# Issue order of the sixteen small matmuls of a tiled DFT stage: column type by column type instead of row tile by row tile

## The chip, the cores and the metric

The kernel runs on one core of one Trainium2 chip. The metric is device time in microseconds (us) of one execution; less is better. Engine names: PE is TensorE (matmuls), PEld its weight loads, DVE is VectorE, ACT is ScalarE, POOL is GpSimd, SP is SyncE, which here only issues transfers. L323 is line 323 of the kernel.

## The reference

```python
def reference(x, filt_r, filt_i, w_gate, w_val, w_out):       # x: 8 batches x 3008 x 256
    X = np.fft.rfft(x, axis=1)
    y = np.fft.irfft(X * (filt_r + 1j * filt_i)[None], n=3008, axis=1)
    t = y.reshape(8 * 3008, 256).astype(np.float32)            # 24064 tokens
    return (np.maximum(t @ w_gate, 0) * (t @ w_val)) @ w_out   # 256 -> 1536 -> 256
```

## The kernel before

A spectral filter along the sequence is followed by a gated feed-forward network (FFN). The kernel spreads the FFN over 564 steps of 1.30 us, each with two matmuls into `psV`, two into `psG` and four into `psO`, and hangs the filter's work for the next batches between these steps. For batches 2 to 7 the filter's first DFT (stage A) is "tiled": POOL loads a chunk of x (`load_chunk`), folds it by symmetry into four half-size inputs (`fold_chunk`, one for each of four column types c), and TensorE does sixteen small fp32 matmuls, one for each pair of row tile q and column type c (`tiled_a`). Each batch has four chunks j, so there are 24 such blocks.

```python
def fold_chunk(b, j):                                   # POOL
    xp = XP[j]
    t = fs.tile([128, 2, 512], FP32, tag="fold", bufs=2, name="fold")
    tt = nc.gpsimd.tensor_tensor
    tt(t, xp[:, 0:2], xp[:, 2:4], op=ALU.add)                        # L309
    tt(xp[:, 2:4], xp[:, 0:2], xp[:, 2:4], op=ALU.subtract)          # L310
    tt(xp[:, 0], t[:, 0], t[:, 1], op=ALU.add)                       # L311: input of c = 0
    tt(t[:, 0], t[:, 0], t[:, 1], op=ALU.subtract)                   # L312: c = 1
    tt(t[:, 1], xp[:, 2], xp[:, 3], op=ALU.add)                      # L313: c = 2
    tt(xp[:, 2], xp[:, 2], xp[:, 3], op=ALU.subtract)                # L314: c = 3
    fold[b, j] = (xp[:, 0], t[:, 0], t[:, 1], xp[:, 2])

def tiled_a(b, j):
    banks = [ps.tile([128, 2, D], FP32, tag=t, name="psF") for t in ("psv", "psg", "fft", "fft")]
    for q in range(4):
        r = 32 * q
        for c in range(4):
            nc.tensor.matmul(banks[q][32 * c:32 * c + 32], WF[r:r + 24, c, :],     # L323
                             fold[b, j][c][r:r + 24], start=True, stop=True,
                             tile_position=(r, 32 * c))
    ...                                  # banks 0, 2 are copied by ACT, 1, 3 by DVE, then stored
...
def load_d(b, z0=0, z1=NZ):              # inputs of the last DFT (stage C), on SP
    for z in range(z0, z1):
        dC = sb.tile([NROW, 8, D], BF16, tag="dC", bufs=6)
        for e in range(2):
            nc.sync.dma_start(dC[48 * e:48 * e + 48], ...)                         # L427
...
# where a batch's work is hung among the FFN steps (e: offset of the four blocks)
for j, e in enumerate((-74, -69, -64, -57)):
    l = (22, 34, 34, 46)[j] if b == 2 else end - 113 + NFT * j
    def next_x(b=b, j=j, l=l):
        hold_gpsimd(yTs[l // NFT + 1][:, 0, 0:8])
        load_chunk(b, j)
        if j:
            fold_chunk(b, j - 1)
        if j == 3:
            fold_chunk(b, j)
    at_step(l, next_x)
    at_step(end + e, lambda b=b, j=j: tiled_a(b, j))
```

## Time and profile before

| | before |
|---|---|
| three timed runs, us | 902.16, 902.18, 902.97 (median 902.18) |
| the run whose trace was taken, us | 897.66, span 895.9, mean granted clock 0.997 |
| PE busy; its share of the chain that ended last | 98%; 84% |
| stage A (psF) in that chain | 3% of the span |
| one stage-A block, first psF start to next psV start | 1.07 us (chunks 0, 2), 1.26 us (chunks 1, 3) |

The execution that was traced took 4.5 us less than the timed ones. "Busy" says which engine could be the bound, the chain says that it is. The time of a single block has to be read from the timeline, because the profile models a matmul's end, as its page says, and only the starts are used here.

### The profile page before, as it was taken

How to read it: one execution, taken by the hardware profiler on the slowest of the kernel's cores; microseconds unless marked ns; L12 is line 12 of the kernel's file. 1: busy time of each engine (PE TensorE's matmuls, PEld its weight loads, DVE VectorE, ACT ScalarE, POOL GpSimd, SP SyncE). 2: the span in 40 equal slices, each digit the busy share in tenths (PEclk: the TensorE clock that was granted, in tenths of full speed). 3: DMA queues.
4: the chain of work that ended last, by engine and by line, in shares of the span. 5: the costliest groups of instructions: out<-in, count | busy, mean ns of one | idle time of the engine just before them, and what ended most of it. 6: DMA issues, size and time to landing. Idle time of an engine off the chain costs nothing.

```text
span 895.9 us, 19186 instructions
## 1 busy us (share of the span) xinstructions
PE 881.8 (98%) x7206; PEld 510.3 (57%) x7206; DVE 569.3 (64%) x873; ACT 499.4 (56%) x891; POOL 363.6 (41%) x361
## 2 busy tenths in 40 slices
PE   7899999999999999999999999999999999999998
PEld 2335555566556665556655666555655566666665
DVE  2636865577665776567766677657766577655553
ACT  3475565556555556555655565555565556555553
POOL 4351399138661376415672167801868000000001
PEclk9999999999999999999999999999999999999999
DMA  9998448534465435463375433763346512241111
GB/s 247 287 230 168 108 141 185 124 82 116 124 155 130 115 104 137 129 139 98 99 176 130 99 101 105 181 133 85 111 139 154 117 32 82 67 88 36 37 30 54
DMA packets 114098, 109.17 MB, mean 122 GB/s; under 512 B 20359, under 2 KB 98599, under 8 KB 113366
## 3 DMA queue, kind: packets, MB, share of 16 engines
q1 hardware_dynamic: 90294, 80.10, 34.6%
q0 software_dynamic: 22992, 26.41, 12.4%
q10 hardware_dynamic: 720, 1.45, 0.4%
q8 instruction: 56, 0.92, 0.4%
q14 instruction: 36, 0.29, 0.1%
HBM read 61.93 MB, written 49.81 MB: 125 GB/s over the span
## 4 chain that ended last, share of the span: by engine, by line
PE 84%; POOL 6%; issue 4%; DMA 3%; DVE 1%; ACT 1%; SPq 0%; POOLq 0%; DVEq 0%
PE psV L467 25%; PE psO L486 25%; PE psG L467 24%; PE psF L323 3%; PE psY L451 2%; PE psD L394 2%; PE psX L364 1%; DMA Fti<-in_filt_i_dram 1%; POOL XP L296 1%; POOL fold L309 1%; POOL XP L310 1%; POOL XP L605 1%; DMA Dbuf<-dsb 1%; PE psJ L520 1%; POOL XP L300 1%
## 5 line engine op out<-in xcount | busy, mean ns | idle before, releaser
L472 DVE SCALAR_TENSOR_TENSOR prod<-psG,vsb 128x512 bf16<-128x512 f32 x564 | 389.2, 690 | 265.9 <-ACT vsb L470 259.1
L470 ACT CAST vsb<-psV 128x512 bf16<-128x512 f32 x564 | 332.1, 589 | 266.1 <-PE psV L467 226.9
L467 PE MATMUL psV<-yT,WvT 128*128 128x512 bf16 x1128 | 336.4, 379 | 0.3 <-ACT vsb L470 0.3
L486 PE MATMUL psO<-WoT,prod 128*128 128x256 bf16 x2256 | 336.4, 273 | 0.0
L467 PE MATMUL psG<-yT,WgT 128*128 128x512 bf16 x1128 | 335.3, 379 | 0.8 <-ACT dsb L401 0.3
L486 PEld LDWEIGHTS <-prod 128*128 128x128 bf16 x2256 | 220.6, 98 | 143.4
L467 PEld LDWEIGHTS <-WgT 128*128 128x128 bf16 x1128 | 110.0, 98 | 135.8 <-issue 2.4
L467 PEld LDWEIGHTS <-WvT 128*128 128x128 bf16 x1128 | 98.4, 98 | 42.1 <-issue 30.8
L258 POOL CAST scr<-yT 128x8 f32<-128x8 bf16 x25 | 4.7, 190 | 263.4 <-ACT yT L456 263.4
L509 POOL DMA_DIRECT2D out_dram<-osb x5 | 2.6, 536 | 196.1 <-ACT osb L499 196.1
L380 DVE TENSOR_TENSOR tt<-psX,Ftr 128x512 bf16<-128x512 f32 x96 | 65.1, 683 | 7.4 <-PE psX L364 7.4
L499 ACT COPY osb<-psO 128x512 f32<-128x512 f32 x92 | 53.9, 586 | 27.4 <-PE psO L486 25.7
L309 POOL TENSOR_TENSOR fold<-XP 128x1024 f32<-128x1024 f32 x24 | 56.5, 2355 | 21.5 <-PE psF L323 20.4
L380 DVE TENSOR_TENSOR uu<-psX,Fti 128x512 bf16<-128x512 f32 x89 | 60.6, 681 | 0.0
L401 ACT CAST dsb<-psD 128x512 bf16<-128x512 f32 x96 | 51.5, 589 | 12.4 <-PE psD L394 12.2
L296 POOL DMA_DIRECT2D XP<-in_x_dram x96 | 56.7, 596 | 1.6 <-issue 0.8
L310 POOL TENSOR_TENSOR XP<-XP 128x1024 f32<-128x1024 f32 x24 | 56.3, 2348 | 1.9
L330 DVE CAST asb<-psF 128x512 bf16<-128x512 f32 x48 | 30.9, 686 | 19.2 <-PE psF L323 14.1
L330 ACT CAST asb<-psF 128x512 bf16<-128x512 f32 x48 | 25.8, 589 | 29.0 <-PE psF L323 29.0
L456 ACT CAST yT<-psY 128x512 bf16<-128x512 f32 x47 | 27.6, 586 | 24.9 <-PE psY L451 24.7
L458 DVE CAST yT<-psY 128x512 bf16<-128x512 f32 x47 | 32.0, 681 | 9.7 <-PE psY L451 9.7
L451 PE MATMUL psY<-M,dC 96*128 96x94 bf16 (+18 forms) x604 | 37.5, 198 | 0.5 <-DMA dC<-Dbuf 0.4
(69 smaller groups left out, 508.2 us busy)
## 6 DMA issues: line engine op xcount, KB each, us to landing
at<-Abuf SPq DMA_DIRECT2D x32, 384.0 KB
dC<-Dbuf SPq DMA_DIRECT2D x64, 192.0 KB
XP<-in_x_dram POOLq DMA_DIRECT2D x48, 256.0 KB, 6.0
Dbuf<-dsb SPq DMA_DIRECT2D x23, 512.0 KB
XP<-in_x_dram POOLq DMA_DIRECT2D x96, 96.0 KB, 2.7
Abuf<-asb SPq DMA_DIRECT2D x96, 96.0 KB
out_dram<-osb SPq DMA_DIRECT2D x69, 94.0 KB
XF<-in_x_dram SPq DMA_DIRECT2D x15, 256.0 KB
```

Source lines behind the costliest of these rows:

```text
L296: nc.gpsimd.dma_start(xp[r:r + 24, 0:4:2, :], _ap(x, (b * N1 * N2 + o) * D, [[N2 * D, 24], [47 * N2 * D, 2], [1, 512]]))
L309: tt(t, xp[:, 0:2], xp[:, 2:4], op=ALU.add)
L310: tt(xp[:, 2:4], xp[:, 0:2], xp[:, 2:4], op=ALU.subtract)
L330: copy(asf[:, :, q, :], banks[q])
L380: nc.vector.tensor_tensor(p, psX, filt, op=ALU.mult)
L401: nc.scalar.copy(dsb[:, a, o:o + 2, :], psD[a])
L451: nc.tensor.matmul(psY[:, o:o + w], dCs[b, n2 // 8][:, n2 % 8, h * 128:(h + 1) * 128], M1[:, n1:n1 + w], start=True, stop=True)
L467: nc.tensor.matmul(pt[:, :W], w[:, h, ft * 128:(ft + 1) * 128], yt[:, h, :], start=(h == 0), stop=(h == 1))
L470: nc.scalar.copy(vsb, psV[:, :W])
L472: nc.vector.scalar_tensor_tensor(prod, in0=psG[:, :W], scalar=0.0, in1=vsb, op0=ALU.max, op1=ALU.mult)
L486: nc.tensor.matmul(psO[:, t % 2], prods[ft][:, t * 128:(t + 1) * 128], WoT[:, ft, :], start=(ft == 0), stop=(ft == NFT - 1))
L499: copy(osb[:, t0 % 2:t % 2 + 1], psO[:, t0 % 2:t % 2 + 1])
```

## The change

The intent, as far as the change itself tells it, is to let consecutive matmuls go to different row tiles, so that no row tile's bank has to be filled before the next begins. The two loops are exchanged and nothing else:

```diff
-        for q in range(4):
-            r = 32 * q
-            for c in range(4):
+        for c in range(4):
+            for q in range(4):
+                r = 32 * q
                 nc.tensor.matmul(banks[q][32 * c:32 * c + 32], WF[r:r + 24, c, :],
                                  fold[b, j][c][r:r + 24], start=True, stop=True,
                                  tile_position=(r, 32 * c))
```

## The prediction

> **What bounds the kernel now.** I read the page's busy shares first, then the chain that ended last, then everything recorded for the changed line (L323, the matmuls of tiled stage A, output psF), and last the timeline of single stage-A blocks. From the page, busy time by engine and the chain by engine and line:
>
> ```profile
> PE 881.8 (98%) x7206; PEld 510.3 (57%) x7206; DVE 569.3 (64%) x873; ACT 499.4 (56%) x891; POOL 363.6 (41%) x361
> ...
> PE 84%; POOL 6%; issue 4%; DMA 3%; DVE 1%; ACT 1%; SPq 0%; POOLq 0%; DVEq 0%
> ```
>
> TensorE is the bound: 98% busy and 84% of the chain. The chain's second line gives psF 3% of the span, about 27 us, so a nanosecond less in a stage-A block is a nanosecond less at the end. But even a stage A that cost nothing would give only 3%. All that is recorded for L323:
>
> ```profile
> L323 PE MATMUL psF<-XP,WF x384: 584/587/612, 131.0 to 696.5; 24*32 24x512 f32 x192
> ...
> L323 PE MATMUL psF<-fold,WF x384: 587/600/612, 131.0 to 696.5; 24*32 24x512 f32 x192
> L323 PEldq EVENT_SEMAPHORE  x72: 51/51/727, 128.9 to 695.9; - x72
> ```
>
> 768 records for 24 blocks (6 batches, 4 chunks each) of 16 matmuls: each fp32 matmul is two passes of some 590 ns. Run one after the other, a block would take 32 x 0.59 = 19 us; it does not. The timeline of PE for a block of chunk 0, then one of chunk 1 (start us, duration, what):
>
> ```profile
> 240.41 0.61 PE L323 MATMUL psF<-XP,WF 24*32 24x512 f32 x1
> 240.42 0.62 PE L323 MATMUL psF<-fold,WF 24*32 24x512 f32 x2
> ...
> 240.51 0.94 PE L323 MATMUL psF<-XP,WF 24*32 24x512 f32 x2
> ...
> 240.96 0.59 PE L323 MATMUL psF<-XP,WF 24*32 24x512 f32 x1
> 241.48 0.60 PE L467 MATMUL psV<-yT,WvT 128*128 128x512 bf16 x2
> ...
> 248.09 0.61 PE L323 MATMUL psF<-XP,WF 24*32 24x512 f32 x1
> ...
> 248.13 0.67 PE L323 MATMUL psF<-XP,WF 24*32 24x512 f32 x2
> 248.22 0.62 PE L323 MATMUL psF<-fold,WF 24*32 24x512 f32 x2
> ...
> 248.36 0.62 PE L323 MATMUL psF<-fold,WF 24*32 24x512 f32 x2
> ...
> 248.83 0.59 PE L323 MATMUL psF<-XP,WF 24*32 24x512 f32 x1
> 249.35 0.60 PE L467 MATMUL psV<-yT,WvT 128*128 128x512 bf16 x2
> ```
>
> In the first block all 16 first passes start within 0.10 us (240.41 to 240.51, under 7 ns apart), the second pass of the last tile starts at 240.96, and the next matmul of the FFN at 241.48: 1.07 us from first to next. The old order already runs all 16 tiles at once. The second block takes 249.35 - 248.09 = 1.26 us, because its first passes come in three clumps: there is a hole after 248.13 and another after 248.24. Every block of chunks 0 and 2 looks like the first, every one of chunks 1 and 3 like the second, except the last two of the first of the six batches. Its last block:
>
> ```profile
> 158.64 0.61 PE L323 MATMUL psF<-XP,WF 24*32 24x512 f32 x1
> ...
> 159.37 0.69 PE L323 MATMUL psF<-XP,WF 24*32 24x512 f32 x2
> ...
> 160.75 0.61 PE L467 MATMUL psV<-yT,WvT 128*128 128x512 bf16 x2
> ```
>
> Here three tiles start at 158.64, and the fourth (column type 3 of row tile 0) waits until 159.37 for POOL's last fold step (L314, which starts at 158.06 and takes 1.26). The 12 tiles of the other rows stand behind it.
>
> [...] four tiles of one row group start under 7 ns apart, each with its own weight load. [...] in the last block nothing passes the tile that waits. [...] here the step is 6.7 ns (0.10 us over 15). [...]
>
> **The change part by part.** Nothing is added or removed: the same 384 matmuls, weight loads, copies and transfers. The comparison of the two programs shows the same instructions on every engine, with the waits moved.
>
> *Blocks of chunks 0 and 2, 12 of them.* Two extra semaphore instructions (51 ns each) stand ahead of row tiles 0 and 1, and both run long before the block starts (238.9 and 239.5 for the block at 240.41). Nothing stalls, 16 starts remain 16 starts: gain 0 for the 11 that have their data.
>
> *Blocks of chunks 1 and 3.* These have four such instructions, one at the first tile of each row, because these tiles wait for two things (their rows' load, and the last user of the bank). For the block at 248.09 the first two run ahead; the last of the four is at 248.2, inside the block. So the two holes are the semaphore instructions of row tiles 2 and 3: 248.13 to 248.22 and 248.24 to 248.36, together 1.26 - 1.07 = 0.19 us. In the old order they come after 8 and 12 matmuls, in the new one after 2 and 3. The old order shows that the queue gets at least four matmuls (and the second instruction after them) ahead of the array, so all four should run ahead and the block become 1.07 us. Five batches with two such blocks: 10 x 0.19 = 1.9 us, all on TensorE's path.
>
> *First batch.* POOL bounds its last two blocks, so what its second block saves is lost in the third's wait. For the last block, the new order puts all tiles of column type 3 at the end: when POOL is done at 159.37, 4 tiles are left instead of 13. The end is then 159.37 + 3 x 0.007 + (241.48 - 240.51 = 0.97) = 160.36 instead of 160.75: 0.39 us, which contains what the block before it gives (4 tiles instead of 13 behind its wait, an estimated 0.16).
>
> *What moves the other way.* Bank 0 is now finished with the 13th tile, not the 4th: its copy by ACT starts about 0.06 us later (9 x 6.7 ns). The next user of that bank is the second FFN step after the block, and the copy ends some 0.5 us ahead of it: free. POOL's loads of the next chunk wait for TensorE at more of their transfers, on a use a whole batch earlier: free.
>
> Sum: 1.9 + 0.4 = 2.3 us of 902.18, so **about 900.0 us**, 0.25% faster.
>
> **The rivals.** (1) *The stalls move with the instructions.* If what held the semaphore instruction in the old order is [...] something that clears only when the block starts, they stall after 2 and 3 tiles just as they did after 8 and 12. Then only the first batch gains: 901.8. For it: the third instruction came at 248.2 though its load was long done, and I can only guess why. Against: the second ran ahead behind four full matmuls. (2) *Serial weight loads.* If tiles of one column group share a path for weights, four in a row would load one after the other, at 27 ns (the distance of the two loads of one tile in a raw record): 16 x 27 = 0.43 us instead of 0.10 until all have started, 24 x 0.33 = 8 us, so 910. Against: the old order also has loads of two row groups in one column within 2 ns of each other. (3) [...] If the old order were serial within a row group, it would save much more; the starts 7 ns apart rule it out. (4) *PSUM or ACT becomes the bound*: the 0.06 us delay is too small against 0.5 us of slack.
>
> **Range and chances.** I give the main line some 65%, rival 1 or a half of it 25%, slower starts 8%. The runs before spread from 902.16 to 902.97, so the upper edge must hold an unchanged kernel: 899.0 to 902.8. No rival reaches 2% (18 us): faster 0.01, same 0.97, slower 0.02.
>
> **What would show it.** Right: blocks of chunks 1 and 3 take 1.07 us from first psF start to next psV start, with 16 starts under 7 ns apart and all four semaphore instructions before the first; those of chunks 0 and 2 are unchanged at 1.07; the last block of the first batch ends about 1.0 us after POOL's step. Wrong: holes after the second and third start (rival 1), starts 27 ns apart (rival 2), or TensorE idle before psV of the second step after a block (rival 4).

The forecast's sum is 1.9 + 0.4 = 2.3 us, and its 6.7 ns for each further tile are the 0.10 us of the block at 240.41 over 15 starts. The words cut from the first rival gave the author's guess of what else might hold the instruction up: how much stands ahead of it, which e3_positions tests.

## The result, and the profile after

In the first set the unchanged kernel took a median of 902.17 us (902.16, 902.18, 902.97 and 901.29), the changed one 897.91 (897.68, 900.4, 896.73, 898.15). The ratio is 0.9957, 95% interval 0.9934 to 0.998: the same within 2%. A ratio here is the mean time of one kernel's fast runs over the mean of the other's of the same rounds, so not quite the quotient of the medians. The predicted 900.0 was 2.1 too high, and 897.91 lies below the range.

First comes the page of the changed kernel, busy time and the chain by engine:

```profile
PE 871.2 (97%) x7086; PEld 507.4 (57%) x7206; DVE 569.3 (64%) x873; ACT 499.3 (56%) x891; POOL 364.4 (41%) x361
...
PE 75%; POOL 6%; issue 5%; DVE 4%; DMA 4%; ACT 4%; SPq 0%; POOLq 0%; DVEq 0%; ACTq 0%
```

Here is a trap. PE seems to have lost 10 us of work and 9 points of the chain. But the count fell from 7206 to 7086 matmuls while the weight loads stayed at 7206: 120 matmul records are missing from this trace, and where one is missing the chain takes another way, over ACT and DVE (4% each of the chain, where they had 1% each). Nothing was saved there. The blocks have to be read instead. This is the timeline of PE over the same chunk-1 block that the prediction shows (start us, duration, what):

```profile
248.23 0.63 PE L323 MATMUL psF<-XP,WF 24*32 24x512 f32 x4
248.25 0.66 PE L323 MATMUL psF<-fold,WF 24*32 24x512 f32 x8
248.31 0.98 PE L323 MATMUL psF<-XP,WF 24*32 24x512 f32 x8
248.71 0.63 PE L323 MATMUL psF<-fold,WF 24*32 24x512 f32 x8
248.76 0.61 PE L323 MATMUL psF<-XP,WF 24*32 24x512 f32 x4
249.30 0.39 PE L467 MATMUL psV<-yT,WvT 128*128 128x512 bf16 x1
```

From 248.23 to 249.30 are 1.07 us, where it was 1.26. The merged rows follow the column types, as the new order has them: four tiles of c = 0, eight of c = 1 and 2, then c = 3 together with its second passes. The two holes are gone. The cause is in what is recorded for L323 in this block, in the kernel before and then in the changed kernel (durations are least, median and greatest in ns, then first and last start):

```profile
L323 PEldq EVENT_SEMAPHORE  x4: 51/51/555, 246.1 to 248.2; - x4
```

```profile
L323 PEldq EVENT_SEMAPHORE  x4: 51/51/556, 246.2 to 247.7; - x4
```

Before, the last of the four semaphore instructions started at 248.2, inside the block that had begun at 248.09. Now it starts at 247.7, ahead of the first matmul at 248.23. In the raw records the second, third and fourth start 1.36, 0.70 and 0.58 us ahead; before, the second, with four tiles ahead of it, came 1.34 us ahead, and the third and fourth, with 8 and 12, came 0.02 and 0.16 us after the block's start. All ready blocks of the changed kernel, of whichever chunk, take 1.073 to 1.074 us.

So the predicted mechanism is there, and still the two traced executions differ by 0.3 us only (spans 895.9 and 895.6), while the timed runs differ by 4. Dividing the span at fixed points of TensorE's work shows where the traces differ:

| stretch | before | after |
|---|---|---|
| start to first tiled block | 131.00 | 130.99 |
| first to fifth block (the first batch of tiled blocks) | 109.41 | 109.57 |
| fifth block to the psV after the last (the other 20 blocks) | 456.62 | 455.80 |
| from there to the start of TensorE's last weight load | 194.21 | 194.21 |
| from there to the end | 4.62 | 5.06 |

The stretch with 20 blocks saved 0.8 us instead of 1.9, the first batch nothing, and the tail lost 0.4. That left three questions: is the timed gain of 4 us real, what gives back 1.1 us among the 20 blocks, and what happens in the first batch?

The first batch depends on a load. This is the timeline of POOL at the fold of the batch's last chunk, before and after:

```profile
149.16 2.35 POOL L309 TENSOR_TENSOR fold<-XP 128x1024 f32<-128x1024 f32 x1 [0.94 <-DMA XP<-in_x_dram]
```

```profile
149.68 2.35 POOL L309 TENSOR_TENSOR fold<-XP 128x1024 f32<-128x1024 f32 x1 [1.46 <-PE psF L323]
```

The bracket is POOL's idle time and what ended it. The second line names PE, but that matmul was long done; the semaphores of the trace show that the last piece of the x chunk landed at 149.44 and released POOL. POOL bounds the last two blocks of this batch: in the kernel before, TensorE idled 1.3 and 0.6 us in them until POOL's L314. A later start of this fold is passed on in full: in e5_new_forced, an experiment below that holds POOL up, it starts 1.45 us later than in the changed kernel's trace (151.13 against 149.68), and the psV behind the batch's last block 1.44 us later (162.32 against 160.88). The traced run of before, the only one I had when I predicted, was an early one.

The given-back 1.1 us is one wait. This is the timeline of PE around 572 us, first in the kernel before, then in the changed kernel; psY is the first work of stage C that uses the fifth batch's `dC`:

```profile
573.71 0.42 PE L451 MATMUL psY<-M,dC 96*128 96x4 bf16 x7
```

```profile
572.56 0.27 PE L451 MATMUL psY<-M,dC 96*128 96x4 bf16 x3
573.72 0.30 PE L451 MATMUL psY<-M,dC 96*128 96x94 bf16 x4 [0.89 <-DMA dC<-Dbuf]
```

Seven matmuls that ran together before now come as three and four, with a wait for the load in between. The load is issued by SP in eight pieces; here is SP's timeline for it, before and after:

```profile
568.19 3.93 SPq L427 DMA_DIRECT2D dC<-Dbuf  x8
```

```profile
568.31 4.93 SPq L427 DMA_DIRECT2D dC<-Dbuf  x8
```

The eight issues took 3.93 us before and 4.93 after; the raw records show that one took 1.20 us instead of 0.46. Beside it lies a fetch of instructions, 16 KB, 0.96 us long: it starts 2.29 us after the first of the eight issues, where it came at 4.58, after all eight, in the kernel before. The page lists its queue as q8, instruction, with 56 packets and 0.92 MB, so 16 KB each. That they bring TensorE's program is inferred: 14,412 of the 19,186 instructions on the page of the kernel before are matmuls and weight loads. Whether such a fetch holds others up is what the experiments had to show.

### The profile page after: what moved, and what is told of

Its sections match the earlier page's. It is cut to its first block, busy times and chain, and to the rows that moved or that the text cites. A ratio compares the mean times of both kernels' runs of the same rounds, so it can differ in the third digit from the quotient of the medians.

```text
span 895.6 us, 19081 instructions
## 1 busy us (share of the span) xinstructions
PE 871.2 (97%) x7086; PEld 507.4 (57%) x7206; DVE 569.3 (64%) x873; ACT 499.3 (56%) x891; POOL 364.4 (41%) x361
## 3 DMA queue, kind: packets, MB, share of 16 engines
q10 hardware_dynamic: 720, 1.45, 0.5%
## 4 chain that ended last, share of the span: by engine, by line
PE 75%; POOL 6%; issue 5%; DVE 4%; DMA 4%; ACT 4%; SPq 0%; POOLq 0%; DVEq 0%; ACTq 0%
PE psG L467 23%; PE psO L486 22%; PE psV L467 21%; DVE prod L472 4%; ACT vsb L470 3%; PE psF L323 2%; PE psD L394 2%; PE psX L364 1%; DMA XP<-in_x_dram 1%; DMA Ftr<-in_filt_r_dram 1%; PE psY L451 1%; POOL XP L296 1%; DMA dC<-Dbuf 1%; POOL fold L309 1%; POOL XP L310 1%
## 5 line engine op out<-in xcount | busy, mean ns | idle before, releaser
L467 PE MATMUL psG<-yT,WgT 128*128 128x512 bf16 x1107 | 330.8, 379 | 6.7 <-ACT dsb L401 0.6
L467 PE MATMUL psV<-yT,WvT 128*128 128x512 bf16 x1030 | 315.2, 380 | 0.3 <-ACT vsb L470 0.3
L258 POOL CAST scr<-yT 128x8 f32<-128x8 bf16 x25 | 4.7, 189 | 262.2 <-ACT yT L456 262.2
```

What stands on the lines that cost most here:

```text
L467: nc.tensor.matmul(pt[:, :W], w[:, h, ft * 128:(ft + 1) * 128], yt[:, h, :], start=(h == 0), stop=(h == 1))
```

## The experiments

Sixteen kernels ran, all with correct results. The ratios are against the unchanged kernel on the same chip; for the e6 runs those were in the main made some minutes earlier, in the set of e4 and e5.

| kernel | chip | median, us (low to high, runs) | ratio (95% interval) |
|---|---|---|---|
| e0_unchanged | 12 | 901.34 (898.05–902.8, 6) | 1.0014 (0.9997–1.0031) |
| e1_changed_again | 12 | 898.17 (897.79–900.57, 5) | 0.9992 (0.9979–1.0005) |
| e2_hoist | 12 | 898.07 (896.16–899.76, 6) | 0.9987 (0.9973–1.0) |
| e3_positions | 12 | 902.37 (one look) | – |
| e4_old_relaxed | 10 | 897.09 (896.39–898.19, 6) | 0.9971 (0.9947–0.9994) |
| e4_new_relaxed | 10 | 896.03 (895.08–897.5, 6) | 0.9958 (0.9934–0.9981) |
| e5_old_forced | 10 | 901.53 (899.14–903.91, 6) | 1.0017 (0.9991–1.0043) |
| e5_new_forced | 10 | 899.01 (898.25–900.1, 6) | 0.9992 (0.9967–1.0018) |
| e6_new_again | 10 | 898.43 (896.9–898.93, 6) | 0.9982 (0.9959–1.0006) |
| e6_new_shift | 10 | 897.0 (895.35–898.85, 6) | 0.9965 (0.9939–0.9991) |
| e6_new_relaxed_shift | 10 | 896.5 (894.77–897.51, 6) | 0.9957 (0.9931–0.9983) |
| e6_old_shift | 10 | 900.21 (899.34–901.28, 6) | 1.0003 (0.998–1.0027) |
| e7_old_forced, e7_new_forced, e7_hoist_forced, e7_old_shift10 | 10 | 900.99, 898.32, 897.62, 903.49 (one look each) | – |

"Old" is the order by row tile, "new" the changed one. Where an expectation names a theory by a letter, its own text says what that theory holds.

### Both kernels again

e0_unchanged is the kernel before without an edit, e1_changed_again the changed kernel without one, on another occasion.

> The unchanged kernel, timed against itself: how far do medians of 5 runs differ for no reason? Theory A (the change is worth 1.9 us plus noise): ratio 1.000, and single runs spread over 3 to 5 us (the profiled run took 897.66 us, the timed ones 901.3 to 903.0), so that a difference of 4 us between two small sets can come by chance. Rival B (the change is worth the whole 4.3 us): the runs of the unchanged kernel stay within 901 to 903, its spread is under 2 us. The trace: blocks of chunks 1 and 3 take 1.26 us from the first start to the next psV, those of chunks 0 and 2 take 1.07.

> The changed kernel again, five rounds. Theory A: 1.9 to 2.3 us below the unchanged kernel of the same rounds (ratio 0.9975 to 0.998). Rival B: 4 us or more below (ratio 0.9955). The trace: all ready blocks 1.07 us; any further difference lies where a transfer lands late (dC ahead of psY, x ahead of the fold in the first batch), at other places than in the first trace of this kernel.

The kernel e0_unchanged and the unchanged runs beside it are the same program: 17 runs with a mean of 899.94 (standard deviation 1.36) against 898.70 for the five of the changed kernel, a difference of 1.24 with a standard error of 0.60. Against the 11 unchanged runs beside them alone it is 0.75 (standard error 0.57): the six of e0_unchanged came out 1.4 us higher than these 11, with the same program, and so far can two such means lie apart for no reason. On the second chip the unchanged kernel has 12 runs with a mean of 900.09 (standard deviation 2.1), the changed one (e6_new_again) 898.30: 1.79, standard error 0.68. Over all later sets the unchanged kernel ran from 897.79 to 904.39, and only 7 of its 29 runs were at 901.29 or above, where all four timed runs of the first set had been. So the 4 us of the first set are for the larger part the level of its runs of the unchanged kernel. That all four were high is not well explained by chance, and what made them so stays open.

### Only the first tile of each row moved (e2_hoist)

```diff
-        for c in range(4):
-            for q in range(4):
+        order = [(q, 0) for q in range(4)] + [(q, c) for q in range(4) for c in range(1, 4)]
+        for q, c in order:
                 r = 32 * q
```

This keeps the row-tile order for 12 of the 16 tiles and takes only the four tiles that carry the waits to the front.

> Old order, except that the first tile of each row tile is issued ahead of all others, so only the four waiting matmuls are moved and the rest stays row by row. Theory A (the gain is that the semaphore instructions run ahead of the array, nothing about row groups): all ready blocks of chunks 1 and 3 take 1.07 us and the time is within 0.5 us of the changed kernel; in the first batch the block that waits for POOL ends 0.06 us later than in the new order, as 12 tiles and not 4 are left. Rival C (cycling through the row tiles itself is faster): these blocks stay above 1.15 us and the time within 0.7 us of the unchanged kernel.

Its chunk-1 and chunk-3 blocks take 1.073 us, as in the changed kernel, and the last semaphore instruction of the same block starts at 248.0, ahead of its first matmul at 248.44:

```profile
L323 PEldq EVENT_SEMAPHORE  x4: 51/51/555, 246.5 to 248.0; - x4
```

So cycling through the row tiles is worth nothing in itself; all of the gain in a ready block comes from issuing the waiting tiles early. The median, 898.07, is that of the changed kernel (898.17).

### How early is early enough (e3_positions)

```diff
+        n = (8, 4, 5, 6, 7, 8)[b - 2]
+        rows01 = [(q, c) for q in range(2) for c in range(1, 4)]
+        rows23 = [(q, c) for q in range(2, 4) for c in range(1, 4)]
+        order = [(0, 0), (1, 0)] + rows01[:n - 2] + [(2, 0), (3, 0)] + rows01[n - 2:] + rows23
+        for q, c in order:
```

In each batch another number n of tiles, 4 to 8, stands ahead of the first tile of row 2, whose semaphore instruction is the third; that of row 3 is the fourth.

> How many tiles may stand ahead of the third semaphore instruction before it stalls? Row tiles 2 and 3 are started after n tiles of rows 0 and 1, with n = 8, 4, 5, 6, 7, 8 in the six batches. Theory D [...]: up to some n between 4 and 7 the blocks of chunks 1 and 3 take 1.07 us, above it they show holes and take 1.15 to 1.25 us; at n = 8 the third instruction runs about 0.02 us after the first start, as in the old order. Rival E (row tile 2 or 3 can't be started ahead at all once a row has all its tiles): all n below 8 give 1.07. Rival F (two tiles is the most): all n from 4 up stall.

With n of 4, 5 and 6 both run ahead (the third some 0.65 to 0.69 us before the block) and the block takes 1.073 us; with 7 only the third does (0.51 us ahead) and the block takes 1.15; with 8 neither, and it takes 1.27. What is recorded for the line of these matmuls (L326 in this kernel) in a block of n = 6, one of 7 and one of 8:

```profile
L326 PEldq EVENT_SEMAPHORE  x4: 51/51/556, 483.2 to 484.7; - x4
```

```profile
L326 PEldq EVENT_SEMAPHORE  x4: 51/51/555, 571.6 to 573.6; - x4
```

```profile
L326 PEldq EVENT_SEMAPHORE  x4: 51/51/556, 678.7 to 680.8; - x4
```

The blocks' first matmuls start at 485.19, 573.61 and 680.65. The last of the four is 0.5 us ahead in the first, level with the start in the second, behind it in the third. So with seven fp32 tiles ahead of it (two passes each, a weight load and a matmul in each: 28 records) a semaphore instruction still runs 0.51 us before the block, and with eight it stalls until the block begins. That refutes the prediction's first rival: the stall belongs to the place in the order of issue and not to the instruction. Each exposed instruction costs 0.08 to 0.12 us, more than the 51 ns of its record. What it is that eight tiles use up and seven do not was not tested.

### Without the wait in the first batch (e4)

```diff
-            for j, e in enumerate((-74, -69, -64, -57)):
+            for j, e in enumerate((-74, -69, -61, -52) if b == 2 else (-74, -69, -64, -57)):
```

The last two blocks of the first batch come three and five FFN steps later, when POOL is done for certain. It was made for the old order (e4_old_relaxed) and the new (e4_new_relaxed).

> Old order, with the last two stage-A blocks of the first batch moved 3 and 5 FFN steps (3.9 and 6.5 us) later, so that TensorE no longer waits for POOL there, however late the x chunk lands. Theory G (most of the spread of the unchanged kernel, and the clock that drops to half for 3.4 us at 160 us in some runs, come from that one wait): runs lie at the lower end of the unchanged kernel's or below, about 896 to 898.5 us, no half-clock period at 160 us, the block takes 1.26 us. Rival H (the spread comes from elsewhere, start-up or late dC loads): the time and its spread are as in the unchanged kernel, 898 to 902.

> New order with the same two blocks moved later. The order alone then makes 12 blocks shorter by 0.19 us: 2.25 us below the old order with the same move (ratio 0.9975), and no more. If the change does something else beside that (rival B: 4 us), it shows here as a larger difference. Theory G also expects this to be the fastest of all, 894 to 896.5 us.

Both are faster than their originals. The old order's mean falls from 900.09 to 897.24, and its runs spread over 1.8 us where the unchanged kernel spreads over 6.3 on the same chip. So the wait for POOL, and behind it for the late load of x, costs some 2.9 us on average and is a large part of what makes the runs differ. In these traces the first batch takes 107.91 (old) and 107.57 (new), a difference of 0.34: 0.19 from its chunk-1 block and 0.15 ahead of a matmul of the next stage (psX, at 183 us). The moved chunk-3 block takes 1.07 in both orders, since at its new place it has only two semaphore instructions; the 1.26 and the twelve shorter blocks that were expected are eleven blocks, or 2.1 us. The means differ by 1.18 (standard error 0.48); the two traces give −0.34 in the first batch, −1.81 in the other 20 blocks (ten blocks, less a new wait of 0.3) and +0.42 in the tail, together −1.73, within the scatter of what was timed. e4_new_relaxed has the lowest median of all kernels, 896.03.

### With the wait forced (e5, e7)

```diff
                     if j == 3:
+                        for _ in range(20 if b == 2 else 0):
+                            hold_gpsimd(WF[:, 0, 0:8])
                         fold_chunk(b, j)
```

Twenty small POOL copies ahead of the last fold make POOL late in every run, whenever the load lands. It was done to the old order, the new, and in the last set also to the order of e2_hoist.

> Old order, with 20 small copies on POOL ahead of the last fold of the first batch, some 3.8 us, so that the late chunk is forced in every run: TensorE waits there for each of POOL's four steps. Theory G: the last block of the batch takes some 4.8 to 5.5 us, the clock drops to half for 3.4 us near 162 us, and the time is 901 to 904 us in every run with a small spread. Rival H: no more than the longer wait itself, about 2.5 us above the unchanged kernel's fast runs, without a half-clock period.

> New order with the same forced delay. Theory I (the new order also helps in late runs: 4 tiles instead of 13 stand behind the last wait, and more matmuls run between the waits, so that the clock does not drop): no half-clock period, 4 to 5 us below the old order with the same delay. Rival J (the clock drops in both orders, as TensorE waits about as long): a half-clock period here too, and the difference is 2 to 2.7 us, 1.9 from the ready blocks and up to 0.8 from the tiles behind the wait.

> Old order with the forced delay of the x chunk once more. Theory I (the clock drops because only one tile runs between POOL's steps): a half-clock period of 3.4 or 6.8 us near 162 us. Rival J (it is chance [...]): in some traces of the old order it is missing.

> New order with the forced delay once more. Theory I: no half-clock period near 160 us (a fifth late trace without). Rival J: one shows here.

> Hoisted order (first tile of each row tile ahead, then row by row) with the forced delay: four tiles run first, then single tiles between POOL's last steps, as in the old order. Theory I: a half-clock period as in the old order, since the wait is passed with single tiles. Rival M (the four tiles at the start, or the semaphore instructions out of the way, are what keeps the clock up): none.

Timed, the forced pair has means of 901.39 and 899.12: 2.3 us apart (standard error 0.78), where theory I expected 4 to 5. In the trace of e5_old_forced the first batch takes 114.23 us, in e5_new_forced 110.73. One part of it is what was predicted. From the start of the first tile of column type 3, which POOL's last fold step (L314) releases, to the next psV are 1.43 us in e7_old_forced and 0.99 in the new order: 0.43, predicted 0.39. Another part was not: TensorE's clock. The view of a stretch of time shows it; the columns are stretch, length, busy us and instruction counts of PE, PEld, DVE, ACT and POOL, then granted clock, DMA share and GB/s. First e5_old_forced, then e5_new_forced, then e7_old_forced, then e7_hoist_forced:

```profile
158.00:164.80 6.80, 6.43 (x43) 1.91 (x43) 2.24 (x4) 2.10 (x4) 3.62 (x3) 0.78 0.15 39
```

```profile
158.00:164.80 6.80, 6.32 (x52) 2.33 (x52) 2.67 (x5) 2.73 (x6) 3.12 (x3) 1.00 0.18 46
```

```profile
158.00:164.80 6.80, 6.15 (x48) 2.24 (x47) 2.48 (x4) 2.42 (x6) 4.19 (x4) 1.00 0.15 39
```

```profile
158.00:164.80 6.80, 6.34 (x53) 2.37 (x52) 2.71 (x5) 2.67 (x6) 2.95 (x3) 1.00 0.21 51
```

PE is "busy" for over 6 us in all four, which is no help. The clock is: 0.78 in the first, because it was halved for some microseconds after the wait; psG there starts 0.82 us after the psV ahead of it (164.97 and 164.15), in e5_new_forced 0.44 (162.76 and 162.32). Among the traces in which POOL was late (its last fold step ended 2 us or more after the block's start), the old order shows this drop in 4 of 5 (e0, e3, whose first batch is close to the old order, e5_old_forced and e7_old_shift10), for 3.4 or 6.8 us, and the new and the hoisted order in 0 of 6. One such drop costs about 2.6 us (114.23 in e5_old_forced against 111.62 in e7_old_forced, the same program without it). My guess, which no run shows, was that the single tiles that the old order leaves between waits bring the drop. e7_hoist_forced speaks against it as the only cause, since that order also waits between single tiles and kept its clock, and e7_old_forced shows that the old order can escape. So that the new order avoids the drop is likely by its frequency, not shown; what decides it in a given run stays open, and rival J, chance, is not excluded. The timed runs of e5_old_forced, expected to spread little, spread over 4.8 us: its two fastest (899.14 and 899.68) have a mean granted clock of 1.000, the other four 0.996 to 0.998. Where in those runs the clock was lost is not on record; five traces, four of them in the new order, also show it halved for 3.4 us in the start-up, at 18 or 40 us (3.41 us from 40.37 on in that of the kernel before).

### The fetch of instructions moved (e6, e7_old_shift10)

```diff
     warm(11)
+    warm(31, 8)
```

These are 31 small matmuls with their weight loads in the start-up, 62 more instructions on TensorE, meant to bring every later fetch to another place of the program; the 46 of e6_old_shift moved the one near 570 us by 6 us (from 4.58 us after the first issue to 1.4 ahead of it). The rival is any other effect of the new order on this load, which should stay. e6_new_again is the changed kernel once more, e6_new_relaxed_shift is e4_new_relaxed with the shift, e6_old_shift has `warm(23, 8)` in the old order, and e7_old_shift10 `warm(10, 8)`; the last two were meant to bring the fetch in among the issues of the fifth batch's load, where it had not been.

> The changed kernel once more, on the chip of this set, beside 11 or so runs of the unchanged kernel: the difference of means. By now I expect 1.9 us from ten ready blocks, plus about 1 us on average where the x chunk lands late (fewer tiles behind the wait, no drop of the clock), less about 1 us for the late dC load: 1.5 to 2.5 us below the unchanged kernel, ratio 0.997 to 0.9985, not 4.3 us. The trace: a wait of 0.8 to 1.4 us at 574 us, no half-clock period at 160 us.

> New order, with 31 tiny warm-up matmuls (62 TensorE instructions) put into the idle start, so that every later fetch of 16 KB of TensorE's instructions falls some 3.7 us earlier. Theory K (in the new order one of these fetches falls among the eight issues of the fifth dC load, one of them is held up, and psY waits 0.8 to 1.4 us for it at 574 us): the fetch near 570 us is gone from that window, all eight issues take 0.33 to 0.47 us, and the wait ahead of psY near 574 us is gone; the time is 0.5 to 1.2 us below that of the new order alone. Rival L (the late dC load has another cause, such as the earlier copies): the wait at 574 us stays.

> The version that the runs point to: new order, the two blocks of the first batch later, and the fetch moved. It beats the new order by what both waits cost, about 1.5 to 2.5 us, and the unchanged kernel by 3 to 5 us: 894.5 to 896.5 us. Against the relaxed new order alone (896.0 us on another chip) only 0.3 us or less is left, as psY waited no more than that there.

> Old order, with 23 such matmuls (46 instructions), so that the fetch that fell 4.6 us after the first issue of the fifth dC load falls some 2 us after it. Theory K: now the old order shows a held-up issue of 1.0 to 1.4 us there and a wait ahead of psY of up to 1.4 us at 574 to 580 us, which none of its four traces had. Rival L: no such wait, as the old order never had it. In time that is at most 1 us, less than the spread between runs.

> Old order with 10 tiny warm-up matmuls (20 instructions). The 46 instructions of the earlier try moved the fetch by 6 us, so 20 move it by 2.6 us, to about 2 us after the first issue of the fifth dC load. Theory K: one of the eight issues is held up (1.0 to 1.7 us instead of 0.46), and the load lands late; TensorE then waits up to 1.2 us ahead of psY, or less if the old order reaches psY later. Rival L: all issues stay below 0.5 us.

SP's issues of that load in e6_new_again, then in e6_new_shift:

```profile
569.25 5.19 SPq L427 DMA_DIRECT2D dC<-Dbuf  x8
```

```profile
571.09 3.92 SPq L427 DMA_DIRECT2D dC<-Dbuf  x8
```

And psY behind it, in PE's timeline of e6_new_again and of e6_new_shift:

```profile
574.88 0.30 PE L451 MATMUL psY<-M,dC 96*128 96x94 bf16 x4 [0.49 <-DMA dC<-Dbuf]
```

```profile
575.06 0.42 PE L451 MATMUL psY<-M,dC 96*128 96x4 bf16 x7
```

With the fetch moved, all eight issues are normal (3.92 us), the seven psY matmuls run as one group, and the wait is gone. The size fits as well, wait by wait:

| trace in the new or hoisted order | wait of psY, us | the 20-block stretch, us |
|---|---|---|
| e1_changed_again | 1.39 | 456.10 |
| after | 1.10 | 455.80 |
| e5_new_forced | 0.77 | 455.47 |
| e7_new_forced | 0.72 | 455.42 |
| e6_new_again | 0.70 | 455.40 |
| e4_new_relaxed | 0.34 | 455.04 |
| e2_hoist, e7_hoist_forced, e6_new_shift, e6_new_relaxed_shift | none | 454.74 to 454.75 |
| old order, seven traces | none | 456.62 to 456.85 |

Row by row the stretch is the 454.75 of the kernels without a wait, plus the wait less 0.05. Against the old order's mean of 456.74 the kernels without a wait save 2.00 us, where 1.9 was predicted; the traces of the first five rows save 1.10 on average and give 0.9 back.

But the fetch alone does not make the wait. In e2_hoist it fell among the issues too, one of them took 1.12 us, and psY did not wait:

```profile
567.47 4.63 SPq L427 DMA_DIRECT2D dC<-Dbuf  x8
```

```profile
572.77 0.42 PE L451 MATMUL psY<-M,dC 96*128 96x4 bf16 x7
```

The same holds for e7_hoist_forced (1.50 us) and for e3_positions (1.65 us, with a fetch 3.46 us after the first issue), though there it was the last of the eight. In e2_hoist psY begins 5.3 us after the load's first issue. In all eight traces in the new order it begins 4.0 to 4.9 us after it, in the other ten 5.2 to 6.3. So the new order also leaves this load about 1 us less, about as much as psY then waits. This is the other effect that was to be tested for, and it stays in e6_new_shift (3.97 us), where the wait is gone: a held-up issue and the shorter time together make the wait. The load's first issue waits for the store into `Dbuf` and comes 7.2 to 8.0 us after that store's issue in the new order, 5.9 to 7.0 in the others. The x load that POOL issues ahead of this store starts 1.81 us after POOL's hold copy (L258) in the new order, 1.03 in the others, in every trace. That this later x load is what slows the store was not tested.

The reverse test failed twice. In e6_old_shift the fetch came 1.4 us ahead of the first issue, in e7_old_shift10 5.35 us after it, never within the window, so these two say nothing for or against; psY came 5.5 and 6.3 us after the first issue there, so that even a hit might not have shown as a wait. A count says more about the issues alone. It takes the last six such loads of each of the 18 traces, and its window was drawn after seeing them: of the 12 loads of `dC` with a fetch of TensorE's instructions that began between 0.3 us before and 3.3 us after the first issue, 11 had an issue of 0.95 us or more, two of them in the old order; of the 96 without, 8 had, and in 5 of these a fetch on the other instruction queue lay there. The load before these six, at 132 us, is left out: all 18 traces have an issue of 1.04 us or more there, without a fetch in the window, so a long issue has other causes too. A fetch that starts in the window nearly always goes with a long issue. Why the new order brings it there is inference, from two measurements: the block's last semaphore instruction starts 0.57 us ahead of the block and no longer 0.16 us into it, and the next fetch of 16 KB starts 0.7 to 1.8 us after the block's start in the new order's traces with an unmoved fetch, 1.9 to 3.1 in the old order's.

In e6_new_relaxed_shift both costs are taken away. Its median, 896.5, is not below that of e4_new_relaxed (896.03), whose wait was only 0.34 us; its one trace shows a start-up 2.9 us longer than that of e4_new_relaxed (134.07 against 131.13), and why was not tested. e6_new_shift is 1.2 us below e6_new_again in the mean (897.08 against 898.30), near the 0.7 of its wait and within the scatter.

## Why the prediction was right and wrong

- **Blocks of chunks 0 and 2, gain 0**: right, 1.07 us before and after. (In the block at 240.41 one of the two semaphore instructions takes 0.47 us and not 51 ns, but it ends 0.99 us ahead of the block.)
- **Blocks of chunks 1 and 3, 0.19 us each**: right, 1.26 to 1.073. Ten blocks were to give 1.9 us; 2.00 were measured where nothing else interferes. The first rival is refuted by e3_positions, the second (serial weight loads) by the starts, and so is the third (an old order that is serial within a row group): its first passes start under 7 ns apart, and e2_hoist gains the same without cycling through the rows.
- **The first batch, 0.39 us**: right as a term (0.43), but read from the one early trace. When the x load lands later, TensorE waits longer there, and in 4 of 5 late traces of the old order the clock dropped in addition.
- **ACT's copy of bank 0 is later but free**: right; the FFN steps behind the blocks show no wait for it, and the ready blocks kept their 1.07 us.
- **The fourth rival** happened in another form than I gave it: TensorE did fall idle before a later matmul, because a `dC` load that had about 1 us less to spare was held up by a fetch of instructions, not because of PSUM or ACT. I had not asked when the next fetch would come. It costs 0.9 us on average in five traces.
- **"POOL's loads of the next chunk wait for TensorE at more of their transfers, on a use a whole batch earlier: free"** is a step that the traces speak against: one such x load starts 0.78 us later in every trace in the new order, and the store and the `dC` load behind it come about 1 us later against TensorE. That the first brings about the second is argued.
- **The tail** grew by 0.4 us in six of the eight traces in the new order: POOL's last instruction to drain its work took 0.25 instead of 0.10 us, and one more fetch lies there. The cause was not tested.
- **The step that failed is the base of the sum, and with it "Range and chances"**: "2.3 us of 902.18", and "The runs before spread from 902.16 to 902.97, so the upper edge must hold an unchanged kernel: 899.0 to 902.8." The mis-sized terms are this level and this spread. Three runs of one occasion gave 902.18 and 0.8 us; later runs of the same program had means of 899.94 and 900.09 and spread over 6.6. From a base of 900.0 the same 2.3 us lead to 897.7, beside the measured 897.91. That they lie so near is partly luck, as the 2.3 us left out the wait of psY (0.9) and the tail (0.4), and what a late x load adds to the gain in the first batch. The later differences, 1.24 and 1.79 with standard errors near 0.65, are both below 2.3 and within two standard errors of it. Why the first set's unchanged runs were high stays open. A warning was in hand: the traced execution had taken 897.66 us, below my low edge, with nothing changed at all.

## What to carry to other kernels

When a matmul has to wait for two things, issue it near the front of its group, so that its semaphore instruction runs while the array is still busy with the work before (here 0.19 us for each block, 1.26 to 1.073); the order of the others is of no account while all of them are ready (1.073 us in e2_hoist too). Before setting a range, compare the time of the traced execution with the timed ones: a disagreement larger than the expected gain is itself the width of the range. After a gain of a microsecond, look for what the earlier instructions now collide with, transfers of instructions included (here one issue of 1.20 us instead of 0.46 beside such a transfer), and for loads that start later because a wait has moved; and read missing records (the matmul count against the weight-load count) before believing a change of the chain.
